# Thirty tiny loads in the load queue of a fused decode block: fifteen behind the second load of keys, fifteen behind the last load of weights

## Chip, cores and metric

The kernel runs on one core of a Trainium2 chip. The metric is the device time of one execution in microseconds; for one core the slowest core is that core. The kernel before takes 185.84 us (median of 2 runs, 185.81 to 185.86). A profiled execution of it gives the trace that the views below are taken from.

## What is computed

One transformer block for one new token per sequence, batch B = 2, width D = 640, all tensors in bf16. A condition c gives six rows of modulation, then comes attention over a cache, then a gated feed-forward layer:

```
mod = (silu(c) @ w_mod).reshape(2, 6, 1, 640)       # sa, ca, ga, sb, cb, gb
h = layernorm(x) * (1 + ca) + sa
q = h @ wq                                          # 32 heads of 192
k, v = the last 1024 positions of k_cache, v_cache  # 2 x 32 x 1024 x 192 each
o = softmax(q k^T * 192**-0.5) v
x = x + ga * (o @ wo)
h = layernorm(x) * (1 + cb) + sb
x = x + gb * ((gelu(h @ w_gate) * (h @ w_up)) @ w_down)
```

Each cached key and value is used once. About 77 MB come from memory, and each is touched by little arithmetic.

## The kernel before

The kernel is written with a small scheduler, `_Sched`. Every operation is recorded with the buffers that it reads and writes; `resolve` works out from them which semaphores it must wait for; `emit` (L106 to L117) then writes each engine's list in the order of recording, with the waits ahead of the instruction. An engine works through its list in order, so an instruction that waits holds up everything behind it on that engine.

All big loads go through one queue, issued by SyncE (SP) with the helper `k_dma` (L289), so that their issues all show as L290 in the profile. The small inputs c and x (L346, L347) and the output store (L685) are issued by ScalarE (ACT) with the same helper. Each big load has a semaphore of its own (`sem_of`, L286).

The loads share one large buffer, the arena (L194). `place` says where each load lies in it, and its order is the order of the loads, seventeen in all: w_mod; w_q; the three pieces of the keys of batch 0 (k 0,0, k 0,1 and k 0,2); then values and keys in turn (v 0,0, k 1,0, v 0,1, k 1,1, v 1,0, v 1,1); w_o; w_gate; w_up; and three pieces of w_down. Each covers all 128 partitions. A load whose place overlaps an earlier load's can only be issued when that one is consumed. This is what `pump` (L333 to L341) does: it issues loads in order until it meets one that must wait, and is called again whenever a load has been consumed. The first call (L343) issues w_mod, w_q, k 0,0 and k 0,1. The next load, k 0,2, takes the place of w_mod, and so its issue waits for the matmuls that use w_mod (L454). The last call, after the values of batch 1, first piece (L593), issues the rest of the weights; after the last piece of w_down, SP has nothing left but to wait for the output store (L698).

The first load is moved ahead of the entry barrier (L689 to L697). Then TensorE and ScalarE work out the modulation (L454, L459), the normalised row and q (L486 to L506). The scores are a product on VectorE over tiles of 16 keys per partition (L512), a partial sum on TensorE with an identity (L524) and a reduction on VectorE (L531); a softmax per batch follows (L536 to L555). The weighted values are matmuls (L575) against masked probabilities (L561). After both batches come w_o (L634), the second normalisation, w_gate and w_up (L655), the gelu product, w_down in three pieces (L675), the last two operations of VectorE (L681, L683) and the store.

Of the kernel before, what the change touches and what calls it, by code (L numbers as in the profile page):

```python
# [8 lines left out]
BF16 = mybir.dt.bfloat16  # L9
# [110 lines left out]
def bass_adaLN_cond__sliding_block_cached__geglu_ffn__decode_kernel(  # L120
# [14 lines left out]
    P = 128  # L135
# [52 lines left out]
    with es:  # L188
        S = _Sched(nc, es)
        sb = lambda name, shape, dt: es.enter_context(nc.sbuf_tensor(name, shape, dt))  # L190
# [10 lines left out]
        for kind, b, t, z in tiles:  # L201
            j0, n = (K_SPLIT if kind == "k" else V_SPLIT)[b][t]
# [66 lines left out]
        go = sb("go", [P, OC], F32)  # L269
        fin = sb("fin", [P, OC], F32)  # L270
        finb = sb("finb", [P, OC], BF16)
        ps = es.enter_context(nc.psum_tensor("ps", [P, 8, 512], F32))

        BK_T = 4
# [10 lines left out]
        sem_c = S.sem("d_c")  # L285
        sem_of = {it: S.sem("d_%s" % "_".join(str(z) for z in it)) for it in place}  # L286
        sem_out = S.sem("d_out")

        def k_dma(dst, src):  # L289
            return lambda e: e.dma_start(dst, src)  # L290
# [5 lines left out]
        def overlap(x, y):  # L296
            (a, m), (b, n) = place[x], place[y]
            return a < b + n and b < a + m

        def keys(it, lo=0, width=None):  # L300
            o, n = place[it]
            width = n - lo if width is None else width
            assert lo + width <= n
            return [("ar", z) for z in range((o + lo) // UNIT, -(-(o + lo + width) // UNIT))]

        def view(it, lo=0, width=None):
            o, n = place[it]
            width = n - lo if width is None else width
            return arena[:, o + lo:o + lo + width]

        def source(it):
            kind = it[0]
            if kind == "wm":
                return w_mod.rearrange("(p k) n -> p (k n)", k=KT)
            if kind == "wq":
                k0, n = WQ_SPLIT[it[1]]
                return A_wq.rearrange("(p k) n -> p (k n)", k=KT)[:, k0 * NQ:(k0 + n) * NQ]
            if kind == "wo":
                t0, n = WO_SPLIT[it[1]]
                return A_wo.rearrange("(p t) n -> p (t n)", t=NT)[:, t0 * D:(t0 + n) * D]  # L320
            if kind == "wg":
                return B_w_gate.rearrange("(p k) n -> p (k n)", k=KT)
            if kind == "wu":
                k0, nk = WU_SPLIT[it[1]]
                return B_w_up.rearrange("(p k) n -> p (k n)", k=KT)[:, k0 * F:(k0 + nk) * F]
            if kind == "wd":
                r0, nr = WD_SPLIT[it[1]]
                return B_w_down.rearrange("(p r) n -> p (r n)", r=FC)[:, r0 * D:(r0 + nr) * D]
            b, (j0, n) = it[1], span[it]
            src = A_k_cache if kind == "k" else A_v_cache  # L330
            return src[b][:, K0:Sk, :].rearrange("h (x j) d -> h x j d", x=XQ)[:, :, j0:j0 + n, :].rearrange("h x j d -> h x (j d)")

        def pump(*consumed):  # L333
            queue["done"].update(consumed)
            while queue["next"] < len(items):
                n = queue["next"]
                it = items[n]
                if not all(x in queue["done"] for x in items[:n] if overlap(x, it)):
                    break
                queue["ops"][it] = S.dma("sp", k_dma(view(it), source(it)), sem_of[it], writes=keys(it), name="ld_%s" % "_".join(str(z) for z in it))  # L340
                queue["next"] += 1  # L341

        pump()  # L343
        wm_dma = queue["ops"][("wm", 0)]
        S.op("pool", lambda e: e.memset(xr[:, :], 0.0), writes=["xr"], name="xr0")
# [102 lines left out]
        for half in range(2):  # L448
# [15 lines left out]
            if half == 0:  # L464
                ln_mod("ln1", 0, 0, hT)
        pump(("wm", 0))

        def out_rows(src, key, dst_t, name):
# [9 lines left out]
        for w, (k0, nk) in enumerate(WQ_SPLIT):  # L478
            def f(e, w=w, k0=k0, nk=nk):
                last = None  # L480
                wv = view(("wq", w)).rearrange("p (k i n) -> p k i n", k=nk, i=NR)
                for kk in range(nk):
                    k = k0 + kk
                    for n in range(NQB):
                        for i in range(NR):
                            last = e.matmul(ps[32 * i:32 * i + B, n, :], lhsT=hT[:, k, 0:RM:RB], rhs=wv[:, kk, i, n * QW:(n + 1) * QW],  # L486
                                            start=(k == 0), stop=(k == KT - 1), tile_position=(0, 32 * i))
                return last
            S.op("pe", f, reads=["ln1_out"] + keys(("wq", w)), writes=[bank(n) for n in range(NQB)], name="q1_%d" % w)
            pump(("wq", w))  # L490
# [177 lines left out]
        for ci, (r0, nr) in enumerate(WD_SPLIT):  # L668
            def f(e, r0=r0, nr=nr):
# [16 lines left out]
              sem_out, reads=["finb"], name="st_out")  # L686
# [8 lines left out]
        moved = body[n0:]  # L695
        del body[n0:]
        body[entry:entry] = moved  # L697
        S.emit("sp", nc.sync, tail=lambda e: e.wait_ge(sem_out, 16))  # L698
        S.emit("pool", nc.gpsimd)
        S.emit("act", nc.scalar)  # L700
        S.emit("dve", nc.vector)
# [43 lines left out]
```

## Time and profile before

| What | Value |
|---|---|
| Median of 2 runs | 185.84 us (185.81 to 185.86) |
| Time of the profiled execution | 184.6 us from its first to its last instruction (the span); no other time of it is given |
| Busy: PE, DVE, ACT, POOL | 106.4, 107.3, 14.4, 6.1 us |
| Data read | 76.88 MB, 417 GB/s over the span |
| Last load issued | 155.7 us |
| Output store issued | 182.80 us |
| Mean granted clock of TensorE | 0.884 |

The profile is a page on one execution. PE is TensorE, DVE VectorE, ACT ScalarE, POOL GpSimd and SP SyncE; a q behind an engine's name means the queue of instructions that it issues DMAs from. Rows of digits cut the span in 40 equal slices, each digit the busy share in tenths. DMA queue q1 is the one that SP's loads use, q10 the one that ACT's DMAs use. The rows of a queue give packets, megabytes and the time that its packets took as a share of 16 DMA engines' span. Rows of waits give who waited for whom: the sum in microseconds, how often, the longest. Rows of the timeline give start, duration, engine, line, operation and tiles, several like instructions joined as "x3" with the time from the first to the end of the last. Rows of DMA issues give the size in KB and the median time from issue to landing. Rows of stretches give the stretch, its length, busy time and instructions of PE, weight loads, DVE, ACT and POOL, then the granted clock, the share of 16 DMA engines and GB/s.

### The profile page before, as it was taken

The numbers are of one execution on the slowest core, as the hardware profiler recorded it, in microseconds if no ns is written. First come the engines' busy times: TensorE is split into PE (matmuls) and PEld (weight loads), VectorE is DVE, ScalarE is ACT, GpSimd is POOL, SyncE is SP. The second block draws the span as 40 slices with busy tenths as digits, with TensorE's granted clock in tenths as the row PEclk, the third lists the DMA queues.
The fourth block names the chain that finished last, engine by engine and source line by source line (L and its number), as shares of the span: only waits on it lengthen the run. The fifth ranks groups of instructions, "written<-read, shape, count | busy, mean of one in ns | idle before, by whom it ended". The sixth has DMA issues, their size and how long they took to land.

```text
span 184.6 us, 1862 instructions
## 1 busy us (share of the span) xinstructions
PE 106.4 (58%) x960; PEld 28.9 (16%) x693; DVE 107.3 (58%) x105; ACT 14.4 (8%) x27; POOL 6.1 (3%) x23
## 2 busy tenths in 40 slices
PE   0019000948663096662499665946662499898833
PEld 0012000120000000001260001500001356405213
DVE  6022200049993488965993999489975838300631
ACT  2041100050000000001000000000001000220410
POOL 8400000000000000000000000000000000000000
PEclk9999955699999859999589999999998559999995
DMA  8999998999898989899898989898999999979991
GB/s 292 492 496 426 426 426 357 442 426 488 368 501 352 501 362 501 384 460 469 384 490 366 490 362 490 373 490 373 479 405 447 506 443 426 426 316 403 434 376 40
DMA packets 2495, 76.99 MB, mean 417 GB/s; under 512 B 310, under 2 KB 440, under 8 KB 568
## 3 DMA queue, kind: packets, MB, share of 16 engines
q1 hardware_dynamic: 2448, 76.87, 97.1%
q8 instruction: 6, 0.10, 0.2%
q10 hardware_dynamic: 40, 0.01, 0.0%
q14 instruction: 1, 0.01, 0.0%
HBM read 76.88 MB, written 0.00 MB: 417 GB/s over the span
## 4 chain that ended last, share of the span: by engine, by line
DMA 58%; DVE 24%; PE 16%; ACT 1%; issue 1%; SPq 0%
DMA arena<-in_A_k_cache_dram 36%; DMA arena<-in_B_w_down_dram 14%; DVE arena L512 14%; PE ps L575 8%; DMA arena<-in_w_mod_dram 8%; DVE S_sb L531 6%; PE ps L524 3%; DVE Em L561 2%; PE ps L454 2%; PE ps L675 1%; DVE negm L541 1%; ACT E_sb L549 1%; PE ps L552 1%; PE ps L545 0%; DVE M L537 0%
## 5 line engine op out<-in xcount | busy, mean ns | idle before, releaser
L524 PE MATMUL ps<-arena,ident_b 128*128 128x512 bf16 x192 | 48.9, 395 | 29.2 <-DVE arena L512 29.2
L512 DVE TENSOR_TENSOR arena<-arena,qbc 128x3072 bf16<-128x3072 bf16 x32 | 54.8, 1750 | 10.2 <-DMA arena<-in_A_k_cache_dram 8.5
L575 PE MATMUL ps<-arena,Em 128*64 128x384 bf16 x256 | 26.1, 374 | 5.6 <-DVE Em L561 5.6
L531 DVE TENSOR_REDUCE S_sb<-ps 128x32 f32<-128x1024 f32 x16 | 19.5, 1218 | 7.1 <-PE ps L524 7.1
L575 PEld LDWEIGHTS ps<-arena,Em 128*64 128x64 bf16 x256 | 16.2, 126 | 30.7 <-DVE Em L561 22.0
L561 DVE TENSOR_TENSOR Em<-E_sb,maskE 128x2048 bf16<-128x2048 bf16 x8 | 18.0, 2282 | 3.9 <-PE ps L575 3.9
L486 PE MATMUL ps<-arena,hT 128*2 128x512 bf16 x60 | 5.1, 517 | 14.0 <-DMA arena<-in_A_wq_dram 14.0
L496 DVE CAST qrow<-ps 128x512 bf16<-128x512 f32 x1 | 0.7, 691 | 17.4 <-PE ps L486 17.4
L539 PEld LDWEIGHTS ps<-ident_f,M 128*1 128x1 f32 x2 | 0.2, 79 | 61.1 <-DVE M L537 61.1
L408 PE MATMUL ps<-Em,ident_b 128*128 128x512 bf16 x41 | 9.3, 379 | 0.0
L641 DVE TENSOR_TENSOR lnt<-ps,modR 128x160 f32<-128x160 f32 x1 | 0.3, 323 | 12.7 <-PE ps L634 12.7
L549 ACT ACTIVATE E_sb<-S_sb,nbias 128x256 bf16<-128x256 f32 x2 | 1.0, 507 | 66.7 <-DVE nbias L547 66.7
L454 PE MATMUL ps<-arena,scT 128*17 128x480 bf16 x40 | 4.2, 602 | 2.1 <-DMA arena<-in_w_mod_dram 2.1
L582 ACT ACTIVATE On<-ps,rden 128x384 bf16<-128x384 f32 x2 | 1.2, 580 | 49.2 <-PE ps L575 49.2
L634 PEld LDWEIGHTS ps<-arena,oT 128*17 128x17 bf16 x192 | 3.3, 91 | 7.4 <-DMA arena<-in_A_wo_dram 7.4
L396 PE MATMUL ps<-ident_b,crow 2*128 2x2 bf16 x5 | 0.4, 177 | 6.5 <-DMA crow<-in_c_dram 6.5
L634 PE MATMUL ps<-arena,oT 128*17 128x160 bf16 x192 | 3.5, 233 | 0.6 <-DMA arena<-in_A_wo_dram 0.6
L417 PE MATMUL ps<-st,selstat 128*128 128x2 f32 x4 | 0.9, 298 | 4.9 <-ACT sqj L413 4.9
L401 DVE CAST X<-xr 128x160 f32<-128x160 bf16 x1 | 0.2, 243 | 5.8 <-DMA xr<-in_A_x_dram 5.8
L486 PEld LDWEIGHTS ps<-arena,hT 128*2 128x2 bf16 x20 | 0.6, 110 | 18.4 <-issue 18.4
L462 DVE TENSOR_SCALAR opc<-modR 128x160 f32<-128x160 f32 x2 | 0.5, 244 | 4.7 <-ACT modR L459 4.7
L655 PE MATMUL ps<-arena,h2T 128*9 128x384 bf16 x40 | 2.0, 326 | 1.9 <-DMA arena<-in_B_w_up_dram 1.3
(86 smaller groups left out, 51.1 us busy)
## 6 DMA issues: line engine op xcount, KB each, us to landing
arena<-in_A_v_cache_dram SPq DMA_DIRECT2D x4, 6144.0 KB, 26.3
arena<-in_A_k_cache_dram SPq DMA_DIRECT2D x3, 6144.0 KB, 37.5
arena<-in_A_wq_dram SPq DMA_DIRECT2D x1, 7680.0 KB, 31.5
arena<-in_A_wo_dram SPq DMA_DIRECT2D x1, 7680.0 KB, 29.2
arena<-in_A_k_cache_dram SPq DMA_DIRECT2D x2, 3072.0 KB, 42.2
arena<-in_w_mod_dram SPq DMA_DIRECT2D x1, 4800.0 KB, 14.2
arena<-in_B_w_gate_dram SPq DMA_DIRECT2D x1, 1920.0 KB, 21.2
arena<-in_B_w_up_dram SPq DMA_DIRECT2D x1, 1920.0 KB, 22.8
```

The costliest lines, as they stand in the source:

```text
L408: last = e.matmul(ps[:, BK_T, :], lhsT=ident_b[:, :], rhs=Em[:, 0, 0:512 // H, :].rearrange("p j h -> p (j h)"), start=True, stop=True)
L454: last = e.matmul(ps[32 * i:32 * i + RM, half, 0:MH].rearrange("p (m n) -> p m n", n=DR), lhsT=scT[:, k, :], rhs=wv[:, 3 * half:3 * half + ...
L486: last = e.matmul(ps[32 * i:32 * i + B, n, :], lhsT=hT[:, k, 0:RM:RB], rhs=wv[:, kk, i, n * QW:(n + 1) * QW], start=(k == 0), stop=(k == K ...
L512: S.op("dve", lambda e: e.tensor_tensor(out=kt, in0=kt, in1=qbc[:, b, :].unsqueeze(1).broadcast_to([P, JC, Dh]), op=ALU.mult), reads=[("qb ...
L524: last = e.matmul(o_ap, lhsT=ident_b[:, :], rhs=kt[:, :, t * GC:(t + 1) * GC], start=(t == 0), stop=(t == NCH - 1))
L531: S.op("dve", lambda e: e.tensor_reduce(out=S_sb[:, b, 2 * JC * pair:2 * JC * (pair + 1)], in_=ps[:, 2 * z:2 * z + 2, :].rearrange("p k (j ...
L541: S.op("dve", lambda e: e.tensor_reduce(out=negm[:, b, :].rearrange("p (h x) -> p h x", x=XQ), in_=ps[0:1, BK_T, 0:P].rearrange("p (h x) - ...
L549: S.op("act", lambda e: e.activation(out=E_sb[:, b, :], in_=S_sb[:, b, :], func=ACTF.Exp, scale=SCALE, bias=nbias[:, b:b + 1], accum_out=d ...
L561: S.op("dve", lambda e, z=z, j=j: e.tensor_tensor(out=Em[:, z, :, :], in0=E_sb[:, b, j:j + JE].unsqueeze(2).broadcast_to([P, JE, H]), in1= ...
L575: last = e.matmul(ps[64 * i:64 * i + 2 * H, BK_O, 0:ON], lhsT=Em[:, z, 2 * jp:2 * jp + 2, :].rearrange("p j h -> p (j h)"), rhs=view(it, l ...
L634: last = e.matmul(ps[32 * i:32 * i + RM, 2, 0:DR], lhsT=oT[:, t, :], rhs=wv[:, t, i, :], start=(t == 0), stop=(t == NT - 1), tile_position ...
L655: last = e.matmul(ps[32 * i:32 * i + GM, bk, 0:FT], lhsT=h2T[:, k, 0:RM:2], rhs=wv[:, k, i * FT:(i + 1) * FT], start=(k == 0), stop=(k == ...
```

## The change

A tile `tiny` of 128 partitions with 2 x 15 x 16 elements and a semaphore are added. A function issues fifteen loads on SP: the n-th, with n from 15 down to 1, copies the first 16 elements (32 bytes) of the first n rows of w_down to n partitions. `pump` calls it right after the issue of k 0,1 and again right after the issue of the last piece of w_down. At the end SP waits for all thirty (30 x 16 counts) ahead of its wait for the store. Nothing reads the tile.

```diff
+        tiny = sb("tiny", [P, 2, 15, 16], BF16)
...
+        sem_tiny = S.sem("d_tiny")
...
+        def tiny_loads(z):
+            for n in range(15, 0, -1):
+                S.dma("sp", k_dma(tiny[0:n, z, n - 1, :], B_w_down[0:n, 0:16]), sem_tiny, name="tiny%d_%d" % (z, n))
+
         def pump(*consumed):
...
                 queue["next"] += 1
+                if it in (("k", 0, 1), ("wd", 2)):
+                    tiny_loads(0 if it[0] == "k" else 1)
...
-        S.emit("sp", nc.sync, tail=lambda e: e.wait_ge(sem_out, 16))
+        S.emit("sp", nc.sync, tail=lambda e: [e.wait_ge(sem_tiny, 16 * 30), e.wait_ge(sem_out, 16)])
```

## The prediction

> **What bounds the kernel now.** I read the page first, the DMA queues and the slices, then the chain of waits, then the load queue's own waits and its timeline, and last a table of stretches at the very end. The page says that the 16 DMA engines are the bound.
>
> ```profile
> span 184.6 us, 1862 instructions
> DMA  8999998999898989899898989898999999979991
> DMA packets 2495, 76.99 MB, mean 417 GB/s; under 512 B 310, under 2 KB 440, under 8 KB 568
> q1 hardware_dynamic: 2448, 76.87, 97.1%
> q10 hardware_dynamic: 40, 0.01, 0.0%
> DMA 58%; DVE 24%; PE 16%; ACT 1%; issue 1%; SPq 0%
> ```
>
> The load queue q1 is busy for 97.1% of 16 engines' span, and no slice but the last falls below 7 tenths. So every microsecond that the slowest engine loses moves the last weights back. The chain gives DMA only 58%: it walks through VectorE where a load's issue waited for a buffer, but the queue had other loads in it meanwhile. The next view, the load queue's own waits and its timeline, shows how much room the issues have.
>
> ```profile
> SPq L290 <- PE ps L454: 16.0, 1, 16.0
> SPq L698 <- DMA out_dram<-finb: 28.4, 1, 28.4
> ```
>
> ```profile
> 0.80 0.33 SPq L290 DMA_DIRECT2D arena<-in_A_wq_dram  x1
> 1.18 17.80 SPq L290 DMA_DIRECT2D arena<-in_A_k_cache_dram  x3
> 37.58 0.54 SPq L290 DMA_DIRECT2D arena<-in_A_v_cache_dram  x1
> ...
> 154.38 0.33 SPq L290 DMA_DIRECT2D arena<-in_B_w_up_dram  x1
> 154.75 1.39 SPq L290 DMA_DIRECT2D arena<-in_B_w_down_dram  x3
> ```
>
> The row at 1.18 holds three issues: k 0,0 and k 0,1 at once, and k 0,2 only at about 18.45 (1.18 + 17.80 less its own 0.53), after the 16.0 us wait for the matmuls of L454. After the last load, at 156.1 (154.75 + 1.39), SP only waits 28.4 us for the output store. Those are the two places where the tiny loads go. The issues' table and the stretches at the end show how the last loads land.
>
> ```profile
> arena<-in_B_w_down_dram SPq DMA_DIRECT2D x1, 1280.0 KB, 25.5
> arena<-in_B_w_down_dram SPq DMA_DIRECT2D x1, 480.0 KB, 26.2
> arena<-in_B_w_down_dram SPq DMA_DIRECT2D x1, 160.0 KB, 26.1
> ```
>
> ```profile
> 179.00:179.50 0.50, 0.00 (x0) 0.00 (x0) 0.50 (x1) 0.00 (x0) 0.00 (x0) 0.81 1.02 394
> 179.50:180.00 0.50, 0.00 (x0) 0.00 (x0) 0.01 (x1) 0.00 (x0) 0.00 (x0) 0.50 0.46 179
> 180.50:181.00 0.50, 0.50 (x37) 0.50 (x40) 0.00 (x0) 0.00 (x0) 0.00 (x0) 0.50 0.31 115
> 181.50:182.00 0.50, 0.50 (x44) 0.49 (x32) 0.00 (x0) 0.00 (x0) 0.00 (x0) 0.50 0.00 0
> ```
>
> With issues at 154.75, 155.2 and 155.7 the three parts of w_down land at 180.3, 181.4 and 181.8. In the stretches (the last two columns are DMA share and GB/s) all engines are busy until 179.5, fewer than half of them (0.46 of 16, about 7) until 180.0, about 5 until 181.0, none after 181.5. So the engines do not finish together: more than half of them are done some 2 us before the last one, and the kernel waits for the last one.
>
> **The change part by part.** Nothing is removed and nothing is moved; 30 loads of n rows of 32 bytes (n = 15 to 1, twice), one semaphore and one end wait are added. No other instruction reads their destination.
>
> *Issues of the first set.* They stand behind k 0,1 (issued by about 2.3: 1.18 plus two of 0.53 and gaps) and ahead of k 0,2. One issue costs between 0.33 us (w_q) and 0.66 (the output store on ACT's queue, the dearest on few partitions), with some 0.05 between issues (1.39 for three of 0.43). I take 0.55, the price of the c load on 2 partitions (0.54) rounded up: 15 x 0.60 = 9.0 us, SP free at 11.3; by the dearest 15 x 0.71 = 10.7, free at 13.0. Queued behind them on SP are the issue of k 0,2 and all later loads. That one cannot leave before 18.45 anyway, so the cost is nothing, hidden by the 16.0 us wait; 5 us of it remain at the dearest price. If that cover were gone there is a second: k 0,1 lands only at about 47.8 (the longest issue to landing is 46.0), so the queue stays full until about then, and 15 issues would have to take 2.8 us each ((45 - 2.3) / 15) before it ran dry.
>
> *Transfers of the first set.* They stand in q1 behind k 0,1 and ahead of k 0,2. In bytes they are nothing: 120 rows of 32 bytes. What counts is packets on one engine. The page's 40 packets of q10 are the two input loads (2 and 8 rows), the store (16 rows) and so 14 completion packets where three full-width loads would have had 48: a load on few rows uses few engines. The worst engine has thus up to 15 rows and 15 completions in a set. Price of one: in the DMA view of the last 7 us,
>
> ```profile
> q10 hardware_dynamic: 24, 0.00, 0.3%
> ```
>
> 24 packets of the store take 0.3% of 16 x 7 us, 0.34 us, so 14 ns each. A tiny load is two packets, 28 ns, and 15 of them 0.42 us on the engine that has them all. From below: if the kernel's last engine is one that few of the loads touch, or the loaded ones are among the half that finish 2 us early, nothing shows at the end. From above: the third part of w_down lands 0.4 us behind the second (181.8 less 181.4), so completions on one engine can follow at 0.41 us; were the tiny loads spaced like that, 15 would cost 6.2 us. But those 0.41 us are full of data (160 KB at 417 GB/s are 0.39), which leaves about 0.02 for a completion, close to the 14 ns. I take the 28 ns, the row it is nearest to. Which engines are the late ones no view tells, so of 0 to 0.42 I take the middle, +0.2.
>
> [...]
>
> *Issues of the second set.* From 156.1, 15 x 0.60: done at 165.1, by the dearest 166.8. Behind them on SP is only the end wait, which ends at 184.5. Cost nothing, hidden by the 28.4 us.
>
> *Transfers of the second set.* In q1 they stand behind the last weights, so they delay no load. They begin on each engine when it is done, 181.5 on the last one, and add 0.42 there: done by about 182.2 with the landing of 181.8. The output store is issued only at 182.80 and lands at 184.5; the new wait on the tiny loads' semaphore is met 2.3 us before that. It bites from 2.7 us a set (184.5 less 181.8), 0.18 us each. Cost nothing.
>
> *Memory and semaphore.* 960 bytes per partition of its own and one more wait on SP at the end, which is met early: nothing, at most the 0.05 of a gap.
>
> Sum: span 184.6 + 0.2 = 184.8. The median of the two runs is 185.84, 1.2 us over the profiled span, and I carry that over: **186.0 us**.
>
> **Rivals.**
>
> *The tiny loads go one behind the other on an engine (slower).* The place is the ring of the engine that has all 15; the price is 0.41 us each at the most. First set: 6.2 us on that engine, and at the end 4.2 to 6.2, as it was early by 2 or not. Second set: 6.2 less the 2.7 of room, 3.5 more. That gives 193.5 to 195.5. For over 2% (3.7 us) it needs about 0.3 us each (first set 4.5, of it 2.5 to 4.5 seen, second 1.8); at 0.1 us each the first set costs up to 1.5, the second nothing: 185.8 to 187.3. For it: no row of before has short packets with completions between them in series on q1. Against: the 0.41 us that are full of data.
>
> *SP is held by too many loads in flight (slower).* The most that the timeline shows in flight is 6 (w_o, w_gate, w_up and three of w_down at 156). If a seventh had to wait, two tiny loads would go out at 3, three more as w_mod, w_q and k 0,0 land, and the other ten only from 47.8, at 0.48 each (0.43 and a gap): k 0,2 would leave at 52.6, with 1 us to its first bytes (the first load needed that), and the queue would stand empty for about 5.8 us: 191.6. For it: nothing but that no row has more. Against: issues with 6 in flight take the same 0.43 us as any.
>
> *The spread of the engines gets smaller (faster).* The tiny loads shift engines against each other; if that made the late ones meet fewer delays, all the 2 us of spread could go: 183.9 at best. Half of it would be 184.9. Against: the early engines run without a gap until 179.5, and a delay put on some engines takes none from the others. This reaches 1%, not 2.
>
> *The change does nothing at all.* The loaded engines are all early ones: 185.8. It is an end of my own case.
>
> **How the numbers follow.** As forecast, loads at a few tens of ns each: 0.80, own range 185.7 to 186.4. One behind the other: 0.11, spread from 186.4 to 195.5, about half of it below 188.5. SP held: 0.04, 191.6. Smaller spread: 0.05, 183.9 to 185.7. A range of 185.0 to 188.4 holds the first case, most of the smaller spread and half of the serial case, and leaves out about 0.12. A measurement of this kernel can tell 2% from no change, 182.1 to 189.6. Over it lie SP held and under half of the serial case: slower 0.09. Nothing but an unnamed effect gives more than 2% of gain: faster 0.01. The rest, 0.90, is the same.
>
> **What would show it.** Right: 15 issues on SP between 2.3 and 11 to 13, k 0,2 still issued at about 18.45; 15 more from 156.1 to 165 or 167; some 480 more packets under 512 B (240 rows and as many completions); w_down landing at 180.3 to 180.7; the store still issued within 0.5 us of 182.80; the end wait still put down to the store. Wrong: an issue of a tiny load far over 0.7 us, or k 0,2 issued after 18.5 (SP held); k 0,2's landing or the last weights 1 us or more later with the issues on time (one behind the other); the end wait put down to the tiny loads (second set over 0.18 us each); a share of DMA at 179.5 to 180.0 well over 0.46 with an earlier end (smaller spread).

## The result and the profile after

The changed kernel takes 187.07 us (187.01 to 187.14, 2 runs) against 185.84: a ratio of 1.0067, 95% interval 1.005 to 1.0083. It is slower by 1.2 us, less than the 2% bound. The forecast was 186.0 with a range of 185.0 to 188.4, so the time lies in the range, but it lies above the 185.7 to 186.4 that the likeliest case allowed, and the loss is six times the 0.2 us that the sum gave. The views follow in the order of those of before. Line numbers shift by 2 to 8: the helper's issues are now L292, the end wait is L706. First the page:

```profile
span 185.8 us, 1890 instructions
DMA packets 2975, 77.00 MB, mean 414 GB/s; under 512 B 790, under 2 KB 920, under 8 KB 1048
q1 hardware_dynamic: 2928, 76.88, 96.9%
```

There are 480 more packets under 512 bytes (790 less 310) as forecast, the same bytes, and a span longer by 1.2 us. Next SP's own waits, its timeline, and the durations of the tiny loads' issues (in ns: shortest, median, longest):

```profile
SPq L706 <- DMA out_dram<-finb: 17.2, 1, 17.2
SPq L292 <- PE ps L462: 9.8, 1, 9.8
```

```profile
1.19 1.26 SPq L292 DMA_DIRECT2D arena<-in_A_k_cache_dram  x2
2.49 5.66 SPq L292 DMA_DIRECT2D tiny<-in_B_w_down_dram  x15
17.97 0.54 SPq L292 DMA_DIRECT2D arena<-in_A_k_cache_dram  x1
...
157.00 1.40 SPq L292 DMA_DIRECT2D arena<-in_B_w_down_dram  x3
158.44 10.16 SPq L292 DMA_DIRECT2D tiny<-in_B_w_down_dram  x15
```

```profile
L292 SPq DMA_DIRECT2D tiny<-in_B_w_down_dram x30: 252/329/2825, 2.5 to 168.1; - x30
```

The first set is issued by 8.2, and SP still waits 9.8 us before k 0,2, which leaves at 17.97, no later than before. The second set takes 10.2 us, one issue of it 2.8, but SP still waits 17.2 us for the store. So SP delays nothing. Then the landings of w_down, and the end in stretches (last columns: DMA share and GB/s):

```profile
arena<-in_B_w_down_dram SPq DMA_DIRECT2D x1, 1280.0 KB, 24.5
arena<-in_B_w_down_dram SPq DMA_DIRECT2D x1, 480.0 KB, 25.2
arena<-in_B_w_down_dram SPq DMA_DIRECT2D x1, 160.0 KB, 25.1
```

```profile
179.00:179.50 0.50, 0.42 (x12) 0.03 (x4) 0.00 (x0) 0.00 (x0) 0.00 (x0) 1.00 1.00 407
179.50:180.00 0.50, 0.00 (x0) 0.00 (x0) 0.45 (x1) 0.00 (x0) 0.00 (x0) 1.00 0.76 300
180.50:181.00 0.50, 0.00 (x0) 0.00 (x0) 0.22 (x1) 0.00 (x0) 0.00 (x0) 1.00 0.64 249
181.50:182.00 0.50, 0.37 (x25) 0.40 (x29) 0.00 (x0) 0.00 (x0) 0.00 (x0) 0.50 0.29 87
```

The first part of w_down lands at 181.5 (157.00 + 24.5) instead of 180.3. Some engines are done before 180 as they were before, but twelve (0.76 of 16) are busy from 179.5 to 180 instead of seven, and ten from 180.5 to 181 instead of five. The loss is a wider spread of the engines, and the kernel waits for the last one.

Where the spread opens shows in the DMA view of the stretch 46.3 to 52, just after the first set has its turn in the queue. Before:

```profile
DMA packets 52, 2.43 MB, mean 427 GB/s; under 512 B 2, under 2 KB 2, under 8 KB 2
```

And after:

```profile
DMA packets 82, 2.14 MB, mean 375 GB/s; under 512 B 38, under 2 KB 38, under 8 KB 38
```

In the same 5.7 us 0.29 MB fewer move, although the issues were on time. In the trace's packet records the tiny rows and completions take 9 ns each, but the next row of keys on their engine, 1.82 us long elsewhere, takes 3.74 us on the engine with fifteen of them and 3.10 on the one with ten: 0.128 us for each tiny load. The price does not begin with the first of them. If the packets are sorted to engines by their times, the engines with up to four tiny loads have a next row of the usual 1.82 us, those with five to seven one that is 0.08 to 0.43 us longer, and from eight on it is 0.11 to 0.13 us for each. The trace of the first set alone gives the same steps.

The engine with ten was late already in this trace: its k 0,1 lands at 48.04, that of the others by 46.87. The last landings of the loads behind it move on in the same steps as the others, so it is the last engine to the end, at 183.06 where the last one before was at 181.84. Its 1.28 us, ten times 0.128, are about the 1.2 us that the kernel lost; that the two agree so closely holds for this trace only (see "Which engines").

### The profile page after: what moved, and what is told of

It reads as the page before. It is cut to its first block, busy times and chain, and to the rows that moved or that the text cites. A ratio compares the mean times of both kernels' runs of the same rounds, so it can differ in the third digit from the quotient of the medians.

```text
span 185.8 us, 1890 instructions
## 1 busy us (share of the span) xinstructions
PE 106.9 (58%) x958; PEld 29.2 (16%) x693; DVE 107.4 (58%) x105; ACT 14.4 (8%) x27; POOL 6.1 (3%) x23
## 3 DMA queue, kind: packets, MB, share of 16 engines
q1 hardware_dynamic: 2928, 76.88, 96.9%
## 4 chain that ended last, share of the span: by engine, by line
DMA 58%; DVE 23%; PE 17%; ACT 1%; issue 1%; SPq 0%
DMA arena<-in_A_k_cache_dram 37%; DMA arena<-in_B_w_down_dram 13%; DVE arena L520 13%; PE ps L583 9%; DMA arena<-in_w_mod_dram 8%; DVE S_sb L539 6%; PE ps L532 4%; DVE Em L569 2%; PE ps L462 2%; PE ps L683 1%; DVE negm L549 1%; ACT E_sb L557 1%; PE ps L560 1%; PE ps L553 1%; DVE M L545 0%
## 5 line engine op out<-in xcount | busy, mean ns | idle before, releaser
L494 PE MATMUL ps<-arena,hT 128*2 128x512 bf16 x60 | 6.1, 593 | 14.4 <-DMA arena<-in_A_wq_dram 14.4
L683 PE MATMUL ps<-arena,aT 128*25 128x80 bf16 (+1 forms) x96 | 1.8, 264 | 2.2 <-DMA arena<-in_B_w_down_dram 2.2
```

Source lines behind the costliest of these rows:

```text
L683: last = e.matmul(ps[32 * i:32 * i + m, BK_OT, CY:CY + OC], lhsT=aT[:, 32 * fc + a:32 * fc + a + m], rhs=wv[:, i, h, :], start=(fc == WD_S ...
```

## The experiments

The completion theory: each load of the first set, a row with a completion behind it, holds its engine for about 0.12 us, and the engine that ends last decides the loss; the second set is free. The rivals: the second set or the end wait (end theory); the short rows as such (row theory); the one semaphore that all share; SP's issues. All kernels below were timed beside the kernel before on the same chip (185.68 to 185.79 us there). In each the end wait is set to the number of its tiny loads; where the second set is left out, its call is left out too. The diffs show the rest.

**One set at a time.** The diff of the first, then of the second:

```diff
-                if it in (("k", 0, 1), ("wd", 2)):
+                if it == ("k", 0, 1):
```

```diff
-                if it in (("k", 0, 1), ("wd", 2)):
+                if it == ("wd", 2):
```

> Only the first set of fifteen tiny loads is kept. Completion theory (each load of the first set holds its engine for about 0.13 us, not 0.028, and the engine with ten of them is the kernel's last): 187.07 us, within 0.15 of the changed kernel. End theory (the second set, behind the last weights, delays the store or the end wait): back at 185.84.

Measured: 187.0 us, ratio 1.006 (1.0047 to 1.0074).

> Only the second set is kept. Completion theory: 185.84 us within 0.15, although SP issues the second set slowly, because nothing stands behind it. End theory: 187.07.

Measured: 185.86 us, ratio 1.0004 (0.9996 to 1.0013). Its issues of the second set and its end wait:

```profile
157.17 9.43 SPq L292 DMA_DIRECT2D tiny<-in_B_w_down_dram  x15
```

```profile
SPq L706 <- DMA out_dram<-finb: 17.8, 1, 17.8
```

The whole loss is the first set's. The second is issued nearly as slowly as in the changed kernel and costs nothing; the end theory falls. The time of the first set alone is as expected; the condition beside it, that the engine with ten is the kernel's last, its trace does not show (see "Which engines").

**Rows or completions.** One load with sixteen rows on each engine, and fifteen loads with one row on each:

```diff
-            for n in range(15, 0, -1):
-                S.dma("sp", k_dma(tiny[0:n, z, n - 1, :], B_w_down[0:n, 0:16]), ...)
+            S.dma("sp", k_dma(tiny[:, z, 0:4:2, :], B_w_down[0:P, 0:64].rearrange("p (a b) -> p a b", a=2)[:, :, 0:16]), ...)
```

> The first set becomes one load of 128 partitions with two rows of 32 bytes in each: sixteen rows on every engine but one completion; no second set. Completion theory: one completion of 0.13 us more on every engine, 185.9 to 186.1. Row theory (it is the short rows, not the completions, that are dear): 16 x 0.13 = 2.1 us on every engine, 187.9.

Measured: 185.91 us, ratio 1.0006 (0.9997 to 1.0014).

```diff
             for n in range(15, 0, -1):
-                S.dma("sp", k_dma(tiny[0:n, z, n - 1, :], B_w_down[0:n, 0:16]), ...)
+                S.dma("sp", k_dma(tiny[0:16, z, n - 1, :], B_w_down[0:16, 0:16]), ...)
```

> Fifteen loads of 16 rows each in place of the first set, so that every engine should have fifteen rows and fifteen completions; no second set. Completion theory and row theory: 15 x 0.13 = 1.9 us on every engine, 187.8 at the end, and the earliest engine late by 1.9 as well. If the loss came from the loads being spread unevenly over the engines, an even spread costs less than the 1.2 us of the changed kernel.

Measured: 188.17 us, ratio 1.0126 (1.0111 to 1.014). The stretch 46.3 to 52 of this kernel:

```profile
DMA packets 105, 1.75 MB, mean 306 GB/s; under 512 B 69, under 2 KB 69, under 8 KB 69
```

Now 0.68 MB are missing, at 427 GB/s 1.6 us of all engines. In the trace the first engine completes k 0,2 at 62.47 instead of 60.72: 1.75 us, 0.12 a load. Sixteen rows behind one completion cost nothing that can be told from zero; fifteen rows with a completion each cost 2.4. That is 0.5 more than 15 x 0.124: in the packet records the next row of keys is longer by 1.5 to 2.3 us, not equally on all engines, and by 2.28 on the engine that lands k 0,1 last, which stays the last to the end. The row theory falls. A load's beginning and its completion always come together in these runs; what speaks for the completion is how they land in the run of two rows below.

**The shared semaphore.** The same first set with fifteen semaphores, and fifteen loads of two rows:

```diff
-        sem_tiny = S.sem("d_tiny")
+        sem_tiny = [S.sem("d_tiny%d" % z) for z in range(15)]
...
-                S.dma("sp", k_dma(tiny[0:n, z, n - 1, :], B_w_down[0:n, 0:16]), sem_tiny, ...)
+                S.dma("sp", k_dma(tiny[0:n, z, n - 1, :], B_w_down[0:n, 0:16]), sem_tiny[n - 1], ...)
```

> The first set alone, each of its fifteen loads with a semaphore of its own. Completion theory (each row with its completion holds its own engine for about 0.12 us): 187.0 us as with one semaphore. Shared-semaphore rival (120 counts on one semaphore from many engines stand in each other's way): back at 185.8 to 186.0.

Measured: 186.99 us, ratio 1.0053 (1.0037 to 1.007).

```diff
-                S.dma("sp", k_dma(tiny[0:n, z, n - 1, :], B_w_down[0:n, 0:16]), ...)
+                S.dma("sp", k_dma(tiny[0:2, z, n - 1, :], B_w_down[0:2, 0:16]), ...)
```

> Fifteen loads of two rows in place of the first set: 30 counts instead of 120, on two engines. Completion theory: two engines late by 15 x 0.124 = 1.9 us, all others as before, the share of DMA engines near the end as before with two of them moved; the end is 185.8 if these two were early ones and up to 187.7 if one was the last. Shared-semaphore rival: a quarter of the 1.2 us, 186.1, with no engine late by more than 0.5.

Measured: 185.96 us, ratio 1.001 (1.0001 to 1.0018). In its trace thirteen engines complete k 0,2 from 60.54 to 61.17, as before, and three at 62.43, 62.72 and 62.95, where before it was one (62.34). The price is paid on the engine and not at the semaphore, and two engines that were early can lose 1.8 us with nearly no trace at the end. The semaphore records show how: the packets of the fifteen loads start 6 ns apart, but on each of the two engines their completions land one behind the other, 0.18 us apart (on one 46.49, 46.66, 46.84 and so on to 48.98).

**Which engines.** Fifteen loads of eight rows (the same line with 8 in place of 2):

> Fifteen loads of eight rows in place of the first set: half of the engines late by 1.9 us, the other half untouched. If the kernel's last engine is always the same one, the runs stand close together, at 185.9 or at 187.8. If it changes from run to run, as the wide scatter of the first set alone (186.36 to 187.30) suggests, the runs scatter over 185.9 to 187.9.

Measured: 187.88 us (187.76 to 188.15), ratio 1.0111 (1.0097 to 1.0125). With half of the engines late the whole 1.9 us shows in every run. That means only that one of the late engines is always among the eight. The traces show that it is not always the same one. In the changed kernel the engine that lands k 0,1 last has ten tiny loads and stays the last; in the first set alone it has two, its next row takes the usual 1.82 us, and others overtake it. What makes it late is something else: by the times a 16 KB packet of the instruction queue (q8) ran on it, from 43.28 to 44.25 in the changed kernel, and the row behind that took 1.46 us instead of 0.91; the same stands at 43.13 in the trace before. More such packets follow until the end. After one of them, at 151.49 in the first set alone, the last landing moves on by 19.15 us over w_o, where the usual step is 18.1: another engine has become the last. So in these traces which engine ends last goes with where these packets fall, too; that they make the wider scatter of the first set alone (186.37 to 187.28) is a guess, as no run varied them.

**More of them.** Thirty loads ahead of k 0,2:

```diff
-            for n in range(15, 0, -1):
-                S.dma("sp", k_dma(tiny[0:n, z, n - 1, :], B_w_down[0:n, 0:16]), ...)
+            for y in range(2):
+                for n in range(15, 0, -1):
+                    S.dma("sp", k_dma(tiny[0:n, y, n - 1, :], B_w_down[0:n, 0:16]), ...)
```

> The first set twice over, 30 loads ahead of the third load of keys; no second set. Completion theory: twice the delay, with a step of 0.25 us from engine to engine, 3.7 us on the worst, so 188.0 to 189.5. If SP is held by loads in flight, as in the second set, its issue of the third load of keys comes late; should it come after 46 us the queue runs empty and the time goes over 190.

Measured: 188.87 us, ratio 1.0164 (1.015 to 1.0178). SP is held, as its timeline and, for 13 to 20 us, the durations of the issues show:

```profile
2.46 33.67 SPq L292 DMA_DIRECT2D tiny<-in_B_w_down_dram  x30
36.17 1.74 SPq L292 DMA_DIRECT2D arena<-in_A_k_cache_dram  x1
38.51 4.88 SPq L292 DMA_DIRECT2D arena<-in_A_v_cache_dram  x1
```

```profile
L292 SPq DMA_DIRECT2D tiny<-in_B_w_down_dram x3: 4482/4485/4487, 10.8 to 19.8; - x3
```

An issue takes 4.48 us there. That is close to twice the 2.27 us that one row of w_q holds an engine (18.1 us from the landing of w_mod to that of w_q, 8 rows on each engine), and a tiny load brings two packets; whether the two numbers belong together, and what holds SP, was not shown. An estimate, from the issues and landings so far, with 8 rows and a completion on an engine for each big load and two packets for each tiny one: some 70 rows and completions are still to come on the fullest engine when it begins, here (at 10.8) and in the second set of the changed kernel (at 162.3). K 0,2 is issued 18 us late and that costs nothing that shows: the time is within the 188.0 to 189.5 that the completion theory gave, and k 0,1, issued at 1.84, takes 45.9 us to land, so the queue is not empty before k 0,2 comes at 36.17.

**Data between them.** The first set on ScalarE's queue, and sixteen-row loads one by one behind the big loads:

```diff
-                S.dma("sp", k_dma(tiny[0:n, z, n - 1, :], B_w_down[0:n, 0:16]), ...)
+                S.dma("act", k_dma(tiny[0:n, z, n - 1, :], B_w_down[0:n, 0:16]), ...)
...
         out_rows(modR[:, 5, :], ("modR", 1), go, "go")
+        tiny_loads(0)
```

> The first set is issued by ScalarE on its own queue, after the modulation, so that its packets take turns with packets of the big loads; no second set. If the 0.12 us is a waiting time of one queue that data of another can fill: 185.8 to 186.0. If it holds the whole engine: 187.0, as from SP.

Measured: 185.87 us, ratio 1.0005 (0.9996 to 1.0013). The packet records show the turns: from 22.06 on an engine that has tiny packets takes one of them, a row or a completion, and then a whole row of a big load. So here too big data stands between the tiny packets.

```diff
-            for n in range(15, 0, -1):
-                S.dma("sp", k_dma(tiny[0:n, z, n - 1, :], B_w_down[0:n, 0:16]), ...)
+            S.dma("sp", k_dma(tiny[0:16, 0, z, :], B_w_down[0:16, 0:16]), ...)
...
-                if it in (("k", 0, 1), ("wd", 2)):
-                    tiny_loads(0 if it[0] == "k" else 1)
+                if it not in (("wm", 0), ("wd", 2)):
+                    tiny_loads(queue["next"] - 2)
```

> The fifteen loads of 16 rows again, on the same queue, but one behind each of fifteen big loads (from that of w_q to the second piece of w_down) instead of in a row; no second set. If the 0.12 us is paid by each load wherever it stands in the queue: 15 x 0.12 on every engine, 188.2 as in a row. If it is paid only because tiny loads follow one another, and the data of the next big load fills it: 185.8 to 186.1.

Measured: 186.22 us, ratio 1.0025 (1.0013 to 1.0036), neither of the two. The stretch 46.3 to 52 of this kernel:

```profile
DMA packets 60, 2.48 MB, mean 435 GB/s; under 512 B 9, under 2 KB 9, under 8 KB 9
```

The dip is gone. 0.5 us over fifteen loads are 0.036 us each (0.016 to 0.045 by the interval), a quarter of what the same loads cost in a row, and the interval holds the 0.028 of the prediction. On the other queue the first set costs nothing that shows.

**Longer rows.** Fifteen loads of 16 rows of 2 KB, then of 4 KB:

```diff
-            for n in range(15, 0, -1):
-                S.dma("sp", k_dma(tiny[0:n, z, n - 1, :], B_w_down[0:n, 0:16]), ...)
...
+            for n in range(15):
+                o = 9 * HS + 1024 * (n // 8)
+                S.dma("sp", k_dma(arena[16 * (n % 8):16 * (n % 8) + 16, o:o + 1024], A_wq[0:16, 0:1024]), ...)
```

> Fifteen loads of 16 rows of 2048 bytes (other weights, into a free part of the arena, so that a later load of keys also waits for them, which it does late enough): 0.49 MB more, 15 x 75 ns = 1.1 us more data on every engine. If a row and its completion have a shortest period of 0.124 us that data hides in: 15 x 0.124 = 1.9 us, 188.2 as with rows of 32 bytes. If the completion costs 0.12 us on top of the data: 1.1 + 1.9 = 3.0, 189.2. If a completion behind a row this long is free: 1.1, 187.0.

Measured: 189.02 us, ratio 1.0169 (1.0156 to 1.0182).

> As the loads of 2 KB rows, with rows of 4096 bytes: 0.98 MB, 15 x 0.15 = 2.3 us more data. If what a completion costs shrinks with the length of the data ahead of it (0.12 us behind 32 bytes, 0.08 behind 2 KB by the landings): 15 x 0.04 = 0.6 on top, 188.7. If it stays at 0.12: 2.3 + 1.9 = 4.2, 190.0. If it is 0.08: 3.5, 189.3.

Measured: 190.99 us, ratio 1.0267 (1.025 to 1.0283), beyond all three. The 2 KB run looks like data and completion added up, but the 4 KB run is 1.0 us slower than even that. The packet records say why: a row took 0.11 and 0.30 us (medians), not the 75 and 150 ns reckoned with, which makes 1.9 and 4.3 us for the fifteen on an engine. All these loads read the same 16 rows of w_q and write 16 partitions at a time, unlike the big ones; whether that makes them slower, or the completions between them do, the two runs don't tell. So what a completion costs behind rows of this length stays open.

## Why the prediction was right, and where it was not

- **What bounds the kernel**, and that the last engine sets the end: right (q1 is busy for 96.9%, and the last landing at 183.06 instead of 181.84 is the 1.2 us). The loss is a wider spread of the engines.
- **Issues of the first set** cost nothing: right, and cheaper than forecast (5.7 us for fifteen, not 9.0).
- **Transfers of the first set**: the term that was mis-sized. The step "24 packets of the store take 0.3% [...] so 14 ns each. A tiny load is two packets, 28 ns" took how long a packet shows as busy for how long it holds an engine. In a row of eight or more each tiny load holds it for 0.11 to 0.13 us, so the span from nothing to 0.42 us was from nothing to 1.9, and the loss 1.2. The 28 ns fit only with data between the loads: 0.036 us each when spread out. The row by which I chose, the third part of w_down 0.4 us behind the second, showed a completion behind eight rows of data; no row of before showed a completion straight behind another load's, and there they land 0.18 us apart, not 0.02.
- **The middle of the range** for the unknown engine was low too: 1.2 of at most 1.9 us were paid, two thirds. In the profiled run the last engine had ten of the fifteen loads. In the first set alone, with the same loss, the engine that was late beforehand had two, so that the loss came out as just ten loads' worth is in part chance.
- **Issues and transfers of the second set** cost nothing: right (1.0004 alone). One issue took 2.8 us, which the sum did not have. In the trace the last weights land at 183.06, the last tiny load completes at 185.08 and the store at 185.75, so of the 2.7 us of room 2.0 were used and not the 0.4 of the sum.
- **Rivals.** The case forecast as likeliest did not occur in its size; the range of 185.0 to 188.4 held because it also took in half of the first rival. What happened is the first rival, one behind the other, at 0.12 us instead of up to 0.41; the text gave 185.8 to 187.3 for 0.1 us each, and that held, as did its sign, the last weights 1 us or more later with the issues on time. The second happened where nothing stood behind it: SP was held (one issue 2.8 us), but not at the seventh load, as the first set's fifteen went out behind four big loads in 5.7 us; what held it was not shown. The third, a smaller spread, was the opposite of what came.

What about a completion takes the 0.12 us was not tried further, nor why the first four in a row cost nothing that shows. The runs show that it is not the row alone (sixteen rows behind one completion: ratio 1.0006), not the semaphore (fifteen of them: 1.0053) and not SP (k 0,2 issued at 17.97), that it is paid by the engine (1.92 us on the one with fifteen loads, nothing on those with up to four), and that it all but goes away when data of the same or another queue stands between the loads (0.036 us each, and a ratio of 1.0005).

## What to carry to other kernels

Where the DMA engines are the bound, as here (96.9%), price a small load by what it takes from the engine that finishes last, and ask what stands before and after it in its queue: in this kernel a tiny load in a long row cost its engine 0.12 us, while its two packets show as busy for 9 ns each. Put small loads on the other queue (no loss that shows here, 1.0005), or one at a time between big ones (0.036 us each), or merge them into one load (1.0006). The loads on few partitions loaded few engines (those of two rows made two engines late, those of sixteen all); look at how the engines' ends are spread before deciding what that costs.

## What was not expected of the hardware

- The price of a tiny load's completion shows in no packet of its own (9 ns each) but in the next big packet on the engine, 3.74 us instead of 1.82 behind fifteen of them. Behind up to four it did not show at all.
- Completions of tiny loads in a row landed 0.18 us apart on one engine (46.49 to 48.98 with two rows each), though their packets start 6 ns apart.
- A 16 KB packet of the instruction queue made one engine about 1.5 us late (1.0 us for itself, and 0.5 more in the row behind it), in the kernel before as well.
- SP was held late in the tiny loads: single issues took up to 2.8 us in the changed kernel (from 162.3) and 4.5 with thirty loads in a row (from 10.8), instead of 0.3. Some 70 packets were still to come on one engine both times, by the estimate above; what held SP was not shown.
- An issue on few partitions was not dearer on SP than one on all 128 (0.33 to 0.62 in the changed kernel): where SP is not held, it took 0.25 to 0.44 us in a row of 15 rows to 1, but for the first tiny load of all, 0.7. On 16 rows, each behind a big load, it took 0.43 to 0.68.
